# A memory-recurrent transformer block on one core: half-wide partial sums in the memory's output pass, free tile shapes for token projections, new orders

## The chip, the cores and the metric

The kernel runs on one core of a Trainium2 chip. The metric is device time in microseconds, the median of several runs; less is better. Engines are named as in the profile: PE is the matmul engine (PEld its weight loads), DVE the vector engine, ACT the scalar engine, POOL the general one, SP the engine that issues most DMAs.

## What is computed

Two layers over 2048 tokens of width 448, in bfloat16, each an attention block with a recurrent memory and a gated MLP with a relu gate, both with a residual sum:

```python
def _A_ref(x, mem0, Wq, Wk, Wv, Wo, seg_len):        # 16 heads of 256, M = 8, seg_len = 32
    ...
    mem = mem0
    for s in range(n_seg):                            # 64 segments
        xs = x[:, s * seg_len:(s + 1) * seg_len, :].copy()
        h = jnp.concatenate([mem, xs], axis=1)        # 8 memory rows and 32 tokens
        q = jnp.einsum('btd,dhe->bhte', h, Wq)
        ...                                           # k and v likewise
        scores = jnp.einsum('bhqe,bhke->bhqk', q, k) * scale
        scores = jnp.where(mask[None, None], scores, -1000000000.0)
        p = _softmax(scores, axis=-1)
        o = jnp.einsum('bhqk,bhke->bhqe', p, v)
        o = jnp.einsum('bhte,hed->btd', o, Wo)
        mem = o[:, :M, :].copy()
        outs.append(o[:, M:, :])
    return jnp.concatenate(outs, axis=1)
...
x = x + _A_ref(_layernorm(x, axis=-1), A_mem0, A_Wq, A_Wk, A_Wv, A_Wo, A_seg_len)
x = x + _B_ref(_layernorm(x, axis=-1), B_W_gate, B_W_up, B_W_down)
x = x + _A_ref(_layernorm(x, axis=-1), A_mem0, A_Wq, A_Wk, A_Wv, A_Wo, A_seg_len)
x = x + _B_ref(_layernorm(x, axis=-1), B_W_gate, B_W_up, B_W_down)
```

The memory of a segment is the output of the eight memory rows of the segment before. That is a chain of 64 steps in each layer. The weights are the same in both layers.

## The kernel before

**Weights.** Wq and Wk of a head are multiplied into one matrix `A` (448 x 448 a head), Wv and Wo into one matrix `Bsb`, so that a head's scores are h A h' and its output is p h B. This is done once at the start: `transposes` (L1086), `product` (L1104).

**The chain.** `chain(step)` does one step of the recurrence for both layers at once: layer 1 at segment `step`, layer 2 at segment `step - LAG`, with `LAG = 7`. The memory rows of both layers (and, from step 7, 16 rows of tokens of an even tile that "ride" along) are 32 columns of `mT`. One step has these parts in turn:

- `A` times `mT` (L1268, in tiles of 64 x 32 of the PE array), copied to `Usb`;
- `Usb` turned by matmuls with `Selm` (L1444) into `uTm`;
- scores (L1467), softmax (L1477 to L1484), a turn of the probabilities (L1507), and the weighted sum of the segment's rows (L1534 to L1541) into `YTm`: 56 chunks of 128 x 32;
- the **output pass** (L1307): the 56 chunks times the 56 chunks of `Bsb`, four at once in tiles of 128 x 32, so that four partial sums of 32 rows x 448 columns stand in the four quarters of one bank of partitions;
- the four partial sums added: ACT copies the first (L1322), DVE adds the second and the third (L1324) and the fourth (L1325, into `Ohi`), and `twice` (L1205) copies 64 columns of `Ohi` for the rotation of blocks;
- the **column product** (L1350), a small matmul per block with a selection matrix, which turns `Ohi` into columns; `halves` copies these into `mT` for the next step.

In steps before `LAG` another form is used: the pass in 256 and 192 columns, both halves of a two-term split summed by matmuls (L1334, L1341). Step 7 (`step < SPLIT`, `SPLIT = 8`) has the pass in 256 and 192 columns with the sums by ACT and DVE.

**Token work.** Between the parts of the chain stand the tokens of the tiles of 128: `att_group` (queries times `A`, L1626, in tiles of 64 x 128; scores, L1655; softmax; weighted sum, L1537 and L1541; output projection, L1693, 128 x 128 tiles), and the MLP (`glu_units`, L1715, 64 x 128 tiles; `glu_down`, L1733, 128 x 128 tiles). `copy_any` (L278, L281) is the copy out of PSUM that ACT or DVE may do.

**Orders.** Nothing is scheduled at run time. The operations are recorded, and `ORDER`, a list of numbers, says in which order they go and on which engine (the number modulo 5 is the engine); `BANKS` gives the PSUM bank of each. `FILLS` puts matmuls on a scratch tile at some places of PE's order. Each engine runs its list in order, waiting on semaphores for what other engines must have done.

**Tile shapes.** The PE array can be used as one tile of 128 x 128, two of 64 x 128, four of 128 x 32 or eight of 64 x 32; an operation's `mode` names the shape (0: 128 x 128, 1: 128 x 32, 2: 64 x 128, 3: 128 x 64, 4: 64 x 32). The column product may run in mode 0 or 2, according to what stands before and after it:

```python
if o.mode == 5:
    o.mode = mode if mode in (0, 2) else 0 if after and after.mode == 0 else 2
```

Of the kernel before, what the change touches and what calls it, by code (L numbers as in the profile page):

```python
# [7 lines left out]
ALU = mybir.AluOpType  # L8
# [42 lines left out]
class _Sched:  # L51
# [76 lines left out]
    def schedule(self):  # L128
# [27 lines left out]
        for o, after in zip(order["pe"], order["pe"][1:] + [None]):  # L156
            if o.mode == 5:
                o.mode = mode if mode in (0, 2) else 0 if after and after.mode == 0 else 2
            mode = o.mode
# [98 lines left out]
EV = ("act", "dve")  # L258

# [25 lines left out]
def bass_interleave_layers__memory_aug_recurrent_mem_tr__glu_gated_reglu__prompt_kernel(  # L285
# [474 lines left out]
)  # L760
FILLS = {56: (11, 0, 0), 69: (9, 0, 0), 1306: (7, 2, 0), 1461: (46, 1, 1)}
TURN = (
# [1098 lines left out]
```

## Time and profile before

| | |
|---|---|
| median of 3 runs | 1510.02 us (1508.71 to 1512.96) |
| profiled execution | span 1515.3 us from its first to its last instruction; no other time of it is given |
| PE busy | 1478.4 us, 98% of the span, 37579 matmuls |
| DVE busy | 1109.6 us, 73% |
| ACT busy | 841.0 us, 56% |
| granted clock of PE | 0.997 on average |

The profile is of one execution. Each line of a group gives the code line, the engine, the operation, what is written and read, the shape and the count, then busy time and the mean of one in ns, then the engine's idle time before it and who ended it. Lines of the timeline begin with the start and the duration in us. Matmuls are pipelined: the start of the next tells when the array is free, the duration of one includes its passage through the array.

### The profile page before, as it was taken

Reading aid. Unit: us, or ns where it says so; the run is one execution under the profiler, and the core shown is the slowest. Engines: PE = TensorE matmul, PEld = TensorE weight load, DVE = VectorE, ACT = ScalarE, POOL = GpSimd, SP = SyncE. Lnnn points to the kernel's source line nnn. Section 1 sums busy time; section 2 is a strip of 40 time slices with the busy share of each in tenths; the row PEclk is TensorE's granted clock in tenths of the full one; section 3 lists DMA queues with packets and bytes.
Section 4 is the critical chain, followed back from the end, with each engine's and each line's share of the span. In section 5 each row is a group of like instructions: output and inputs, shape, how many; then the busy total and the mean of one; then the engine's idle time right before and its main releaser. Section 6 shows DMA issues by size and latency. Waiting matters only on the chain.

```text
span 1515.3 us, 83381 instructions
## 1 busy us (share of the span) xinstructions
PE 1478.4 (98%) x37579; PEld 1063.1 (70%) x37579; DVE 1109.6 (73%) x3353; ACT 841.0 (56%) x2383; POOL 60.0 (4%) x240
## 2 busy tenths in 40 slices
PE   8999999999999999999999999999999999999998
PEld 6576766667667776677767777677767676677675
DVE  7655768678776878678776778778777878778774
ACT  6755556556565556555655655555555556545542
POOL 1000000000000000000000000000000000000000
PEclk9999999999999999999999999999999999999999
DMA  9831122222222212212122223213222222213211
GB/s 237 194 89 44 28 43 44 44 37 46 46 39 41 45 32 51 42 31 52 44 42 38 44 44 53 40 35 47 47 44 31 52 43 53 39 41 40 47 27 27
DMA packets 239346, 78.20 MB, mean 52 GB/s; under 512 B 212104, under 2 KB 238992, under 8 KB 238992
## 3 DMA queue, kind: packets, MB, share of 16 engines
q1 hardware_dynamic: 238352, 72.60, 25.2%
q8 instruction: 297, 4.87, 1.4%
q14 instruction: 57, 0.47, 0.1%
q10 hardware_dynamic: 640, 0.26, 0.1%
HBM read 17.68 MB, written 1.84 MB: 13 GB/s over the span
## 4 chain that ended last, share of the span: by engine, by line
PE 87%; DVE 6%; DMA 3%; ACT 2%; issue 1%; SPq 1%; DVEq 0%; POOL 0%
PE psG L1626 14%; PE psG L1693 14%; PE psG L1715 11%; PE psC L1307 11%; PE psC L1268 7%; PE psG L1733 6%; PE psG L1268 5%; PE psG L1104 3%; PE psG L1537 2%; PE psG L1655 2%; PE psC L1467 1%; PE psC L1693 1%; PE psC L1444 1%; DMA UR<-Usb 1%; PE psC L1534 1%
## 5 line engine op out<-in xcount | busy, mean ns | idle before, releaser
L1693 PE MATMUL psG<-Bsb,YT 128*128 128x448 bf16 x1232 | 263.8, 353 | 0.0
L278 ACT ACTIVATE Ug<-psG 64x128 bf16<-64x128 f32 (+2 forms) x424 | 152.7, 374 | 73.6 <-PE psG L1626 64.5
L1307 PE MATMUL psC<-Bsb,YTm 128*32 128x448 bf16 (+2 forms) x4088 | 188.0, 335 | 1.0 <-DVE YTm L281 0.5
L1715 PE MATMUL psG<-G,glu 64*128 64x128 bf16 x5866 | 183.6, 216 | 2.6 <-DMA G<-xn 2.4
L1715 PEld LDWEIGHTS psG<-G,glu 64*128 64x128 bf16 x5866 | 170.3, 94 | 14.5 <-issue 8.6
L1626 PE MATMUL psG<-HT,A 64*128 64x128 bf16 x3424 | 175.8, 217 | 0.3 <-ACT Bsb L278 0.3
L1693 PEld LDWEIGHTS psG<-Bsb,YT 128*128 128x128 bf16 x1232 | 107.3, 97 | 89.0 <-issue 7.7
L1268 PE MATMUL psG<-A,mT 64*32 64x448 bf16 x4564 | 158.8, 350 | 2.8 <-issue 1.9
L1626 PE MATMUL psG<-HX,A 64*128 64x128 bf16 x2568 | 149.9, 217 | 0.0
L1307 PEld LDWEIGHTS psC<-Bsb,YTm 128*32 128x32 bf16 x4088 | 101.4, 97 | 67.2 <-DVE YTm L281 3.2
L281 DVE CAST Ug<-psG 64x128 bf16<-64x128 f32 (+2 forms) x277 | 114.9, 427 | 25.3 <-PE psG L1626 21.3
L1268 PE MATMUL psC<-A,mT 64*32 64x448 bf16 x3276 | 128.8, 351 | 1.0 <-issue 0.6
L1626 PEld LDWEIGHTS psG<-HT,A 64*128 64x128 bf16 x3424 | 116.6, 94 | 8.9 <-issue 5.0
L1324 DVE TENSOR_TENSOR Usb<-psC,Usb 32x448 f32<-32x448 f32 (+2 forms) x122 | 74.4, 610 | 63.7 <-ACT Usb L1322 60.9
L278 ACT ACTIVATE YT<-psG 128x448 bf16<-128x448 f32 x217 | 109.3, 538 | 20.3 <-PE psG L1541 20.0
L281 DVE CAST YT<-psG 128x448 bf16<-128x448 f32 x145 | 88.2, 618 | 41.2 <-PE psG L1541 40.4
L1720 ACT ACTIVATE hG<-psG 128x512 bf16<-128x512 f32 (+1 forms) x123 | 66.7, 543 | 81.6 <-PE psG L1715 78.8
L1268 PEld LDWEIGHTS psG<-A,mT 64*32 64x32 bf16 x4564 | 80.5, 92 | 32.3 <-issue 4.0
L1733 PE MATMUL psG<-glu,hG 128*128 128x448 bf16 x448 | 99.8, 353 | 0.0
L1268 PEld LDWEIGHTS psC<-A,mT 64*32 64x32 bf16 x3276 | 64.9, 93 | 45.4 <-ACT mT L278 2.7
L1626 PEld LDWEIGHTS psG<-HX,A 64*128 64x128 bf16 x2568 | 95.2, 94 | 0.0
L1626 PE MATMUL psG<-l,A 64*128 64x128 bf16 x2807 | 94.4, 216 | 0.0
(274 smaller groups left out, 2755.7 us busy)
## 6 DMA issues: line engine op xcount, KB each, us to landing
Bsb<-in_A_Wq_dram SPq DMA_DIRECT2D x6, 384.0 KB
Bsb<-in_A_Wk_dram SPq DMA_DIRECT2D x6, 384.0 KB
Tsb<-Ohi SPq DMA_DIRECT2D x128, 7.0 KB
UR<-Usb SPq DMA_TRANSPOSE x124, 2.9
X<-in_A_x_dram SPq DMA_DIRECT2D x16, 112.0 KB, 5.6
glu<-in_A_Wo_dram SPq DMA_DIRECT2D x4, 448.0 KB
out_dram<-X SPq DMA_DIRECT2D x16, 112.0 KB
glu<-in_B_W_gate_dram SPq DMA_DIRECT2D x14, 112.0 KB
```

The lines of the kernel that those rows point to most:

```text
L278: return E.activation(out, i, ACT.Copy, scale=1.0 if scale is None else scale)
L281: return E.tensor_copy(out, i)
L1104: i = E.matmul(bk.ap()[row0:row0 + mn, 0:D], lhsT=lhs[:, et, m0:m0 + mn], rhs=rhs[:, et, :], start=(et == 0), stop=(et == 1), tile_positio ...
L1268: i = E.matmul(ub[v].ap()[32 * j:32 * j + 32, 0:D], lhsT=self.mT[rw, b, :], rhs=self.A[rw, b, a0:a0 + D], start=(b == 0), stop=(b == 6), t ...
L1307: x = E.matmul(bo.ap()[32 * j:32 * j + 32, 0:d1 - d0], lhsT=self.YTm[:, q, :], rhs=self.Bsb[:, chunks[q], d0:d1], start=(i == 0), stop=(i ...
L1324: s.add("dve", dv_cost(n), lambda E, e, j=j, a_=a_, part=part: E.tensor_tensor(a_, part(j), a_, ALU.add), r=[bo], w=w, part=(j, 0), **P)
L1537: return E.matmul(ps[:, n * q:n * q + n], lhsT=HR[rows, KM + 128 * q:KM + 128 * q + 128], rhs=PT, start=True, stop=True, tile_position=(b, 0))
L1626: i = E.matmul(ub[v].ap()[:, 128 * n:128 * n + 128], lhsT=self.A[rw, b, a0:a0 + 128], rhs=HT[rw, b, :, 0:SEG] if b < 4 else HX[rw, b - 4, ...
L1693: i = E.matmul(bo.ap()[:, 0:D], lhsT=YT[:, c, :], rhs=self.Bsb[:, 14 * g + c, :], start=(g == 0 and c == 0), stop=(g == 3 and c == 13))
L1715: i_ = E.matmul(two[v].ap()[:, 128 * c:128 * c + 128], lhsT=self.Wgu[rw, b, f0:f0 + 128], rhs=G[rw, b, :], start=(b == 0), stop=(b == 6), ...
L1720: s.add("act", 169 + 0.84 * N, lambda E, e, dst=dst, z=two[0], N=N: E.activation(dst, z.ap()[:, 0:N], ACT.Relu), r=[two[0]], w=[("hG", i, ...
L1733: i_ = E.matmul(bk.ap()[:, 0:D], lhsT=hG[:, c, :], rhs=self.Wd[:, c, :], start=(c == 0), stop=(c == NFC - 1))
```

## The change

Four things change. First, the output pass from step 7 on (`out_pass`): a chunk's 448 columns are taken in two halves of 224, by two of the four tiles, so that the bank holds two partial sums of each half, not four of the full width. There are 28 rounds of four 224-wide matmuls in place of 14 of four 448-wide ones. ACT copies one part of each half and DVE adds the other; `twice` follows the first half. Step 7 takes this form too. Second, the output projection of tokens and `glu_down` (mode 6) take the shape that stands before them if that is 128 x 128 or 128 x 32; in the latter each 448-wide matmul becomes four with 32 columns of weights each (`by_rows`). The column product (mode 7) may take 128 x 128, 128 x 32 or 64 x 128. Third, `ORDER`, `BANKS` and `FILLS` are new: the order of all operations, the engine of many copies, and the order of the loads at the start. Fourth, the probabilities' write also names the tile's first clearing as something it comes after.

```diff
-        for o, after in zip(order["pe"], order["pe"][1:] + [None]):
-            if o.mode == 5:
-                o.mode = mode if mode in (0, 2) else 0 if after and after.mode == 0 else 2
+        for o in order["pe"]:
+            if o.mode in FREE:
+                o.mode = mode if mode in FREE[o.mode] else 0
             mode = o.mode
...
+FREE = {6: (0, 1), 7: (0, 1, 2)}
+
+def by_rows(E, mode, out, lhsT, rhs, **k):
+    if mode != 1:
+        return E.matmul(out, lhsT=lhsT, rhs=rhs, **k)
+    for j in range(4):
+        c = slice(32 * j, 32 * j + 32)
+        i = E.matmul(out[c], lhsT=lhsT[:, c], rhs=rhs, tile_position=(0, 32 * j), **k)
+    return i
...
-FILLS = {56: (11, 0, 0), 69: (9, 0, 0), 1306: (7, 2, 0), 1461: (46, 1, 1)}
+FILLS = {12: (50, 7, 0), 22: (9, 1, 0), 54: (5, 3, 0), 70: (4, 6, 0)}
...
-        for d0, d1 in ((0, 256), (256, D)) if step < SPLIT else ((0, D),):
+        if step >= LAG:
+            self.out_pass(chunks, ykeys, P)
+        for d0, d1 in ((0, 256), (256, D)) if step < LAG else ():
...
-            s.add("act", 169 + 0.84 * n, lambda E, e, a_=a_, part=part: E.activation(a_, part(0), ACT.Copy), r=[bo], w=w, **P)
-            for j in (1, 2):
-                s.add("dve", dv_cost(n), lambda E, e, j=j, a_=a_, part=part: E.tensor_tensor(a_, part(j), a_, ALU.add), r=[bo], w=w, part=(j, 0), **P)
-            s.add("dve", dv_cost(n), lambda E, e, a_=a_, o_=o_, part=part: E.tensor_tensor(o_, part(3), a_, ALU.add), r=[bo] + w, ...)
...
+    def out_pass(self, chunks, ykeys, P):
+        s = self.s
+        n = D // 2
+        bo = self.bank("C", "G")
+        for lo, hi in ((0, 10), (10, 20), (20, 28)):
+            def oo(E, e, lo=lo, hi=hi):
+                for i in range(lo, hi):
+                    for j in range(4):
+                        q = 2 * i + j // 2
+                        d0 = n * (j % 2)
+                        x = E.matmul(bo.ap()[32 * j:32 * j + 32, 0:n], lhsT=self.YTm[:, q, :], rhs=self.Bsb[:, chunks[q], d0:d0 + n],
+                                     start=(i == 0), stop=(i == 27), tile_position=(0, 32 * j))
+                return x
+            s.add("pe", (hi - lo) * 96, oo, r=ykeys + self.B_all, w=[bo], alloc=[bo] if lo == 0 else (), mode=1, **P)
+        for g in range(2):
+            a_, o_ = self.Osum[:, n * g:n * g + n], self.Ohi[0:32, 64 + n * g:64 + n * g + n]
+            part = lambda z, g=g: bo.ap()[32 * (g + 2 * z):32 * (g + 2 * z) + 32, 0:n]
+            s.add("act", 169 + 0.84 * n, lambda E, e, a_=a_, part=part: E.activation(a_, part(0), ACT.Copy), r=[bo],
+                  w=[("Usb", 2 * g)], part=(g, 0), **P)
+            s.add("dve", dv_cost(n), lambda E, e, a_=a_, o_=o_, part=part: E.tensor_tensor(o_, part(1), a_, ALU.add), r=[bo, ("Usb", 2 * g)],
+                  w=["Ohi"] if g == 0 else [("Ohi", 256)], part=(g + 2, 0), **P)
+            if g == 0:
+                self.twice(self.Ohi, "Ohi", "Ohi2", P)
...
-                    i = E.matmul(bo.ap()[:, 0:D], lhsT=YT[:, c, :], rhs=self.Bsb[:, 14 * g + c, :], start=(g == 0 and c == 0), stop=(g == 3 and c == 13))
+                    i = by_rows(E, op[0].mode, bo.ap()[:, 0:D], YT[:, c, :], self.Bsb[:, 14 * g + c, :], start=(g == 0 and c == 0), stop=(g == 3 and c == 13))
...
-                    i_ = E.matmul(bk.ap()[:, 0:D], lhsT=hG[:, c, :], rhs=self.Wd[:, c, :], start=(c == 0), stop=(c == NFC - 1))
+                    i_ = by_rows(E, op[0].mode, bk.ap()[:, 0:D], hG[:, c, :], self.Wd[:, c, :], start=(c == 0), stop=(c == NFC - 1))
...
-                      r=[k_(f"E{c}"), k_(f"rc{c}")], w=[k_(f"P{c}")], **P)
+                      r=[k_(f"E{c}"), k_(f"rc{c}"), k_("P")], w=[k_(f"P{c}")], **P)
```

More of the change, by code (lines that the diff above doesn't have):

```diff
@@ L1297, in chain @@
         ykeys = [(k, c, z) for k in ("YTm", "YTr") for c in range(2) for z in (0, 28)]
-        O, acc = self.Ohi, self.Osum
-        for d0, d1 in ((0, 256), (256, D)) if step < SPLIT else ((0, D),):
+        O = self.Ohi
+        if step >= LAG:
+            self.out_pass(chunks, ykeys, P)
+        for d0, d1 in ((0, 256), (256, D)) if step < LAG else ():
             bo = self.bank("C", "G")
             n = d1 - d0
-            for lo, hi in ((0, 5), (5, 10), (10, 14)) if n == D else ((0, 14),):
+            for lo, hi in ((0, 14),):
                 def oo(E, e, lo=lo, hi=hi, bo=bo, d0=d0, d1=d1):
@@ L1310, in chain @@
                 s.add("pe", (hi - lo) * max(n / 2.4 + 3, 100), oo, r=ykeys + self.B_all, w=[bo], alloc=[bo] if lo == 0 else (), mode=1, **P)
-            part = lambda j, bo=bo, n=n: bo.ap()[32 * j:32 * j + 32, 0:n]
-            if step < LAG:
-                hi, lo = (z[:, 64 + d0:64 + d1] for z in self.HL)
-                s.add("act", 169 + 0.84 * n, lambda E, e, hi=hi, bo=bo, n=n: E.activation(hi, bo.ap()[:, 0:n], ACT.Copy), r=[bo], w=[("Hi", d0)], **P)
-                s.add("dve", dv_cost(n), lambda E, e, hi=hi, lo=lo, bo=bo, n=n: E.tensor_tensor(lo, bo.ap()[:, 0:n], hi, ALU.subtract),
-                      r=[bo, ("Hi", d0)], w=[("Lo", d0)], **P)
-                if d0 == 0:
-                    for w, k in zip(self.HL, ("Hi", "Lo")):
-                        self.twice(w, (k, 0), k + "2", P)
-                continue
-            a_, o_, w = acc[:, d0:d1], O[0:32, 64 + d0:64 + d1], [("Osum", z) for z in (0, 256) if d0 <= z < d1] + [("Usb", 0), ("Usb", 2)]
-            s.add("act", 169 + 0.84 * n, lambda E, e, a_=a_, part=part: E.activation(a_, part(0), ACT.Copy), r=[bo], w=w, **P)
-            for j in (1, 2):
-                s.add("dve", dv_cost(n), lambda E, e, j=j, a_=a_, part=part: E.tensor_tensor(a_, part(j), a_, ALU.add), r=[bo], w=w, part=(j, 0), **P)
-            s.add("dve", dv_cost(n), lambda E, e, a_=a_, o_=o_, part=part: E.tensor_tensor(o_, part(3), a_, ALU.add), r=[bo] + w, w=["Ohi"] * (d0 == 0) + [("Ohi", 256)] * (d1 == D),
-                  part=(3, 0), **P)
+            hi, lo = (z[:, 64 + d0:64 + d1] for z in self.HL)
+            s.add("act", 169 + 0.84 * n, lambda E, e, hi=hi, bo=bo, n=n: E.activation(hi, bo.ap()[:, 0:n], ACT.Copy), r=[bo], w=[("Hi", d0)], **P)
+            s.add("dve", dv_cost(n), lambda E, e, hi=hi, lo=lo, bo=bo, n=n: E.tensor_tensor(lo, bo.ap()[:, 0:n], hi, ALU.subtract),
+                  r=[bo, ("Hi", d0)], w=[("Lo", d0)], **P)
+            if d0 == 0:
+                for w, k in zip(self.HL, ("Hi", "Lo")):
+                    self.twice(w, (k, 0), k + "2", P)
         bc_ = self.bank("C", "G")
@@ L1344, in chain @@
         else:
-            self.twice(O, "Ohi", "Ohi2", P)
             def cols(E, e):
@@ L1349, in cols @@
                 for k in range(4):
-                    i = E.matmul(pk()[:, k, :], lhsT=block(O, k)[0:n], rhs=self.Sel16[0:n, :], start=True, stop=True, **at)
+                    i = by_rows(E, op.mode, pk()[:, k, :], block(O, k)[0:n], self.Sel16[0:n, :], start=True, stop=True, **at)
                 return i
-            op = s.add("pe", 4 * 28, cols, r=["Ohi", ("Ohi", 256), "Ohi2", "Sel16"], w=[bc_], alloc=[bc_], mode=5, **P)
+            op = s.add("pe", 4 * 28, cols, r=["Ohi", ("Ohi", 256), "Ohi2", "Sel16"], w=[bc_], alloc=[bc_], mode=7, **P)
         self.halves(self.mT[:, :, 0:16], pk, 16, bc_, "mTm", ("mTh",), P=P)
@@ L1501, in middle @@
                 s.add("dve", 239, lambda E, e, c=c, b=b: E.tensor_scalar(Pv[:, b, 0:L], m["E"][:, c, 0:L], m["st"][:, 4 + c:5 + c], None, op0=ALU.mult),
-                      r=[k_("Em"), k_("rc")], w=[k_(f"P{c}")], **P)
+                      r=[k_("Em"), k_("rc"), k_("P")], w=[k_(f"P{c}")], **P)
         if m["n"] == "r":
```

9 lines of the change are left out of this document (4 added, 5 removed), and 1075 rows, old and new, of tables (BANKS, ORDER).

## The prediction, before the result

> **What bounds the kernel now.** I read the page's sums first, then busy time by stretch of the span, then what the matmul engine waited for, and last one step of the recurrence in order of time. From the page:
>
> ```profile
> span 1515.3 us, 83381 instructions
> PE 1478.4 (98%) x37579; PEld 1063.1 (70%) x37579; DVE 1109.6 (73%) x3353; ACT 841.0 (56%) x2383; POOL 60.0 (4%) x240
> PE 87%; DVE 6%; DMA 3%; ACT 2%; issue 1%; SPq 1%; DVEq 0%; POOL 0%
> ```
>
> PE is busy for 98% of the span and carries 87% of the chain that ended last. All PE work added is therefore paid, and all that can be won is in the 36.9 us (1515.3 - 1478.4) in which PE idles. Where these lie is in the sums by stretch (PE busy is the second number after the stretch):
>
> ```profile
> 0.00:6.00 6.00, 0.49 (x6) 0.52 (x7) 4.56 (x17) 1.28 (x1) 5.38 (x19) 1.00 0.66 186
> 6.00:70.00 64.00, 63.33 (x740) 39.96 (x738) 48.05 (x111) 50.31 (x104) 2.23 (x6) 1.00 0.95 229
> 70.00:400.00 330.00, 316.57 (x8516) 227.67 (x8516) 228.57 (x713) 180.10 (x538) 12.23 (x50) 0.99 0.25 48
> 400.00:1480.00 1080.00, 1067.52 (x27784) 773.98 (x27777) 815.22 (x2485) 602.11 (x1726) 40.12 (x166) 1.00 0.23 42
> ```
>
> 5.5 us go before the first matmul. The weight products until 70 us lose 0.7, the early steps until 400 us lose 13.4, the long middle loses 12.5, and the rest, 4.8, comes after 1480 us, nearly all behind the last matmul. So some 26.6 us stand between matmuls. The clock is granted in full (0.99 to 1.00), so the clock explains nothing. Who ends PE's waits:
>
> ```profile
> PE psC L1350 <- DVE Ohi L1205: 2.6, 3, 2.0
> PE psG L1715 <- DMA G<-xn: 2.4, 2, 2.2
> PE psG L1268 <- issue: 1.9, 2, 1.2
> PE psG L1467 <- ACT uTm L278: 1.8, 5, 0.6
> PE psC L1534 <- DMA Tr<-Pr: 1.7, 3, 0.8
> PE psC L1467 <- DVE uTr L281: 1.6, 3, 0.9
> ```
>
> No single wait is large. Most are in the recurrence (L1350, L1467, L1268), and DVE ends more of them than ACT.
>
> **The change part by part.** The sum is made on the span of the profiled execution, 1515.3 us. The median of the runs is 1510.02, 0.35% less; I scale the sum by 1510.02 / 1515.3 = 0.9965.
>
> *Output pass, PE.* From step 7 on, 63 steps, 14 rounds of four 448-wide matmuls become 28 rounds of four 224-wide ones. The steps before show both shapes. A steady step, and below it an early one whose pass runs as 14 rounds of 256 and 14 rounds of 192, which is 28 rounds of 224 on average:
>
> ```profile
> 802.41 2.83 PE L1307 MATMUL psC<-Bsb,YTm 128*32 128x448 bf16 x56
> ...
> 805.17 3.30 PE L1715 MATMUL psG<-G,glu 64*128 64x128 bf16 x112
> 805.29 0.53 ACT L1322 ACTIVATE Usb<-psC 32x448 f32<-32x448 f32 x1 [1.52 <-PE psC L1307]
> 805.86 1.27 DVE L1324 TENSOR_TENSOR Usb<-psC,Usb 32x448 f32<-32x448 f32 x2 [1.98 <-ACT Usb L1322]
> ...
> 807.16 0.62 DVE L1325 TENSOR_TENSOR Ohi<-psC,Usb 32x448 bf16<-32x448 f32 x1
> ...
> 807.85 0.24 POOL L1205 COPY Ohi<-Ohi 128x64 bf16<-128x64 bf16 x1 [11.17 <-DVE Ohi L1325]
> 808.31 0.20 PE L1350 MATMUL psC<-Sel,Ohi 64*128 64x16 bf16 x2
> ```
> ```profile
> 71.65 2.87 PE L1307 MATMUL psC<-Bsb,YTm 128*32 128x256 bf16 x112
> 74.45 0.40 PE L1626 MATMUL psG<-HT,A 64*128 64x128 bf16 x8
> ```
>
> From the pass's start to the next start: 805.17 - 802.41 = 2.76 us for 14 wide rounds, 74.45 - 71.65 = 2.80 for 28 narrow ones. That is 0.04 more in each of 62 steps (step 7 was split already): **+2.5 us**. The doubled weight loads hide.
>
> ```profile
> L1307 PEld LDWEIGHTS psC<-Bsb,YTm 128*32 128x32 bf16 x4088 | 101.4, 97 | 67.2 <-DVE YTm L281 3.2 <-issue 0.7 <-DVE uTr L281 0.4
> ```
>
> One load lasts 97 ns, yet 112 loads and 112 matmuls pass in 2.80 us, 25 ns a pair. [...]
>
> *Tile shapes.* Full-width projections in 128x128 tiles:
>
> ```profile
> 1487.76 5.47 PE L1693 MATMUL psG<-Bsb,YT 128*128 128x448 bf16 x28
> 1493.07 0.92 PE L1733 MATMUL psG<-glu,hG 128*128 128x448 bf16 x4
> ```
>
> (1493.07 - 1487.76) / 28 = 0.190 us each. Fourteen rounds at 0.190 are 2.66, and the pass above took 2.76 with one change of tile shape behind it: a change of shape costs 0.10 us. Token projections that now run as four 32-column matmuls are one such 448-wide round, 0.190 again: nothing. (The new order does this for 221 of 1888.) What it is for is fewer changes of shape, but the two instruction orders, counted, have 552 before and 581 after: 29 x 0.10 = **+2.9 us**. In eight steps the small column product after the pass runs as 16 matmuls of 32 columns in place of four. Its cost lies between nothing (four at once) and 12 more at the 25 ns of a pair above, 0.3 us; half of it, times 8: **+1.2 us** (0 to 2.4).
>
> *Behind the output pass.* Before, ACT copies the first part (0.53), DVE adds three (1.27 and 0.62), POOL doubles 64 columns: from the pass's end, 802.41 + 2.83 = 805.24, to the column product at 808.31, 3.07 us. After, ACT copies two half-wide parts, DVE adds one to each, and the doubling needs the first half alone. The step that was split shows such widths:
>
> ```profile
> 182.88 0.37 ACT L1322 ACTIVATE Usb<-psC 32x256 f32<-32x256 f32 x1 [0.52 <-PE psC L1307]
> 183.32 0.87 DVE L1324 TENSOR_TENSOR Usb<-psC,Usb 32x256 f32<-32x256 f32 x2
> ...
> 184.68 0.32 ACT L1322 ACTIVATE Usb<-psC 32x192 f32<-32x192 f32 x1 [1.43 <-DVE Ohi L1325]
> ...
> 185.03 0.74 DVE L1324 TENSOR_TENSOR Usb<-psC,Usb 32x192 f32<-32x192 f32 x2 [0.17 <-ACT Usb L1322]
> ```
>
> Halfway between 256 and 192: ACT 0.345, DVE 0.40. One copy and two adds, the second copy beside the first add, with the 0.05 (805.24 to 805.29), 0.04 and 0.22 (808.09 to 808.31) seen between steps: 0.345 + 2 x 0.40 + 0.3 = 1.45 us. The recurrence is 1.6 us shorter per step, and DVE's load falls by 62 x 1.89 - 63 x 0.80 = 67 us, while ACT's rises by 63 x 0.69 - 62 x 0.53 = 11.
>
> *What that is worth.* PE didn't stand still for these 3.07 us: the order put token work there. Pricing the matmuls that stand between the pass and the column product (0.190 for a full one, and so on), I count a median of 3.3 to 3.6 us before and 2.1 to 2.6 after, so the order takes back some 1.1 of the 1.6. That work now stands in the other gaps of the step; before the next step's first product the quarter point rises from 1.1 to 1.5 us. So the gain isn't 63 x 1.6 = 101 us; it is at most what PE idles between matmuls, 26.6. Some 22 of these can go at the most (26.6 less the DMA rows of the list, 2.4 and 1.7, which stay); nothing is the least, if other work is late next. I take a little more than the middle, **-13 us**: wider gaps in nearly every place, and the engine that ends most waits lighter by 6% (67 of 1109.6).
>
> *The start.* The new order puts 59 filling matmuls before the first weight transposes, where PE waited 5.5 us anyway:
>
> ```profile
> 5.51 0.80 PE L1086 MATMUL psG<-ident,Bsb 128*128 128x128 bf16 x6 [5.51 <-DMA Bsb<-in_A_Wq_dram]
> 6.96 1.38 PE L183 MATMUL psC<-warm 128*128 128x128 bf16 x11
> ```
>
> Eleven took 1.38 us, 0.11 each with the last one's drain; 59 at 0.09 last from 1 to about 6.3 us, so the transposes start 0.8 later, then run without the 20 fills that stood among them. Against that, SP's queue now has three DMA transposes of Wv ahead of the last loads of Wq and Wk:
>
> ```profile
> 31.58 4.41 SPq L1046 DMA_TRANSPOSE glu<-in_A_Wv_dram  x1
> 10.00:20.00 10.00, 9.66 (x125) 6.67 (x125) 7.26 (x17) 7.26 (x15) 0.07 (x1) 1.00 1.10 309
> 30.00:40.00 10.00, 10.00 (x115) 6.58 (x113) 7.20 (x18) 8.11 (x16) 0.00 (x0) 1.00 1.07 188
> ```
>
> Plain loads came at 309 GB/s; in the stretch of the transposes 188. The PE work that needed 7.7 MB delivered now needs 10.7, at about 35 us. At 309 for 9.3 MB and 188 for 1.4, these have landed at 38 us at the earliest and 43 if SP is held up for each as here, 4.4 us. I put the start at **+1.5 us** (-1.5 to +6).
>
> *Sum.* 2.5 + 2.9 + 1.2 + 1.5 - 13 = -4.9: 1510.4 on the profile's scale, times 0.9965: **1505 us**, 0.33% less. 0.3%, 4.5 us, is about what a measurement of this kernel can tell from no change.
>
> **The rivals.**
> 1. *The waits move.* The order shortened the gap as the recurrence shortened; another releaser (ACT's share, which rises, or a transfer) is late next, and PE idles as long as before. For it: the list of waits is flat, with ACT, DMA and issue in it. Against: the gaps grow elsewhere too. Place: the recurrence's matmuls in steps 7 to 69. Price: only 2.5 + 2.9 + 1.2 + 1.5 = +8.1 is left, 1523.4, so 1518 us. It ends slower when less than 3.6 us of idle time goes (8.1 - 4.5).
> 2. *The start starves.* The weights land at 43 us, PE loses 8 us: +6.5 on my sum, 1516.9, so 1511.6. For it: the byte counts; against: other products were put there as cover.
> 3. *DVE's relief goes further.* All 22 us go: 1501.4, so 1496 us. For it: DVE ends most waits; against: the early steps' idle time is partly lack of token work.
> 4. *Weight loads come to light.* If the second half's loads didn't overlap, 14 rounds of 0.097 in 62 steps are 84 us: 1594, so 1589. The 2.80 us row speaks against it. [...]
>
> **How the numbers follow.** Forecast 0.35 (its own range 1500 to 1510: 0.20 faster, 0.15 the same), rival 1 0.27 (0.24 slower, 0.03 the same), rival 2 0.13 (0.02, 0.06, 0.05), rival 3 0.24 (faster), rival 4 0.01 (slower). Faster 0.46, same 0.24, slower 0.30. The range runs from 1492 (rival 3 with the cheap ends: 0 for the column product, -1.5 for the start) to 1523 (rival 1 with the dear ones, 2.4 and 6); it leaves out rival 4 and the combination of rivals 1 and 2.
>
> **What would show it.** In the profile after: the pass's matmuls 224 wide, its start to the next start 2.80 us; one ACT copy and one DVE add to each half, 0.35 and 0.40; from the pass to the column product 1.5 us where PE has nothing else; DVE busy near 1043 us, ACT near 852; PE idle after 70 us near 13 us rather than 26; the first weight transposes near 6.3 us and no idle over 3 us before 75. I am wrong if PE's idle time after 70 us stays over 22 us (rival 1), if PE's list of waits shows several us on the weights (rival 2), or if PE's busy time rises by much more than 7 us (the tile shapes or rival 4).

## The result, and the profile after

The changed kernel takes 1535.86 us (median; 1531.35 to 1538.69), the kernel before beside it 1510.69: the ratio is 1.0169 [1.0151, 1.0187]. It is slower, by 1.7%, where 1505 us was forecast; the range ended at 1523. Run once more later it took 1543.08 us, ratio 1.0199 [1.0179, 1.0219].

The page of the changed kernel: the span, busy time by engine, one of the DMA queues (packets, MB, share of 16 engines' span), and the chain by engine.

```profile
span 1534.8 us, 91834 instructions
...
PE 1494.1 (97%) x41805; PEld 1149.3 (75%) x41805; DVE 1021.3 (67%) x3281; ACT 846.4 (55%) x2442; POOL 60.4 (4%) x249
...
q8 instruction: 330, 5.41, 1.4%
...
PE 92%; DMA 3%; DVE 1%; issue 1%; ACT 1%; SPq 1%; POOL 0%
```

The same queue on the page of before:

```profile
q8 instruction: 297, 4.87, 1.4%
```

PE is still the bound. It has 4226 matmuls more than before (41805 against 37579), but only 15.7 us more busy time, for 19.5 us more span. The row to see, and one that I had passed over, is the queue that carries instructions: 330 packets of 16 KB in place of 297.

The sums by stretch of the changed kernel (PE busy is the second number after the stretch, the granted clock the third from the end):

```profile
6.00:70.00 64.00, 53.18 (x563) 34.63 (x562) 36.76 (x91) 37.42 (x81) 2.97 (x7) 0.96 0.94 221
70.00:400.00 330.00, 321.04 (x9352) 241.29 (x9358) 214.93 (x690) 184.86 (x551) 14.53 (x59) 0.99 0.23 48
400.00:1480.00 1080.00, 1064.46 (x30661) 829.62 (x30647) 738.87 (x2417) 602.65 (x1760) 39.39 (x168) 1.00 0.23 43
```

Until 70 us PE idles 10.8 us, where before it idled 0.7. After that it idles 9.0 and 15.5 us, 24.5 in all, against 13.4 and 12.5 before: nothing gained. PE's waits, the largest first (us in total, times, longest):

```profile
PE psG L1453 <- issue: 2.9, 6, 0.8
PE psG L1271 <- issue: 2.7, 1, 2.7
PE psC L1271 <- DVE A L291: 2.6, 1, 2.6
PE psG L1289 <- issue: 2.3, 1, 2.3
PE psG L1567 <- DVE YTm L292: 1.9, 4, 0.8
```

Before, one of the six largest was "issue", a wait for which the profile shows no releaser. Now three of five are; but two of these three, at L1271 and L1289, are single stops of the start, before 75 us, and their matmuls have a semaphore to wait for. So the list alone doesn't tell. I added up PE's idle time between matmuls, pauses over 40 ns beyond the passing of the matmuls' columns and the time of a change of tile shape, by whether the matmul that ends it has a semaphore to wait for:

```
                        before 75 us        after 75 us
                        all waits     semaphore   no semaphore
before                     3.2          38.6          8.4
changed                   17.4          30.9         22.6
difference               +14.2          -7.7        +14.2
```

The sum is +20.7 of the +19.5 us of span; the rest, -1.2, holds among others the work added and the 4.5 us by which the first matmul, a filling one, starts sooner (at 0.99 us, not 5.51). The split depends a little on how a pause is counted: from start to start, with 0.09 us taken off for a change of shape, the differences are +14.5, -10.2 and +13.3. So two things were lost, of like size: the start, and pauses with nothing to wait for. The relief that was forecast is there too, but smaller.

### The profile page after: what moved, and what is told of

Same layout as the page of the kernel before. It is cut to its first block, busy times and chain, and to the rows that moved or that the text cites. A ratio compares the mean times of both kernels' runs of the same rounds, so it can differ in the third digit from the quotient of the medians.

```text
span 1534.8 us, 91834 instructions
## 1 busy us (share of the span) xinstructions
PE 1494.1 (97%) x41805; PEld 1149.3 (75%) x41805; DVE 1021.3 (67%) x3281; ACT 846.4 (55%) x2442; POOL 60.4 (4%) x249
## 4 chain that ended last, share of the span: by engine, by line
PE 92%; DMA 3%; DVE 1%; issue 1%; ACT 1%; SPq 1%; POOL 0%
PE psG L265 14%; PE psG L1827 13%; PE psG L1453 10%; PE psG L1916 9%; PE psG L1567 8%; PE psC L265 5%; PE psC L1827 4%; PE psC L1453 3%; PE psC L1567 3%; PE psC L1916 3%; PE psG L1738 3%; PE psG L1856 2%; PE psG L268 2%; PE psG L1289 2%; PE psG L1668 2%; PE psG L1645 1%
## 5 line engine op out<-in xcount | busy, mean ns | idle before, releaser
L1453 PE MATMUL psG<-A,mT 64*32 64x448 bf16 x5852 | 194.8, 350 | 3.5 <-issue 2.9
L265 PE MATMUL psG<-Bsb,YT 128*128 128x448 bf16 x831 | 177.4, 352 | 0.0
L1453 PEld LDWEIGHTS psG<-A,mT 64*32 64x32 bf16 x5852 | 101.6, 92 | 62.2 <-issue 10.8
L1567 PE MATMUL psG<-Bsb,YTm 128*32 128x224 bf16 x5264 | 136.2, 259 | 2.9 <-DVE YTm L292 1.9
L1567 PEld LDWEIGHTS psG<-Bsb,YTm 128*32 128x32 bf16 x5264 | 123.0, 97 | 9.3 <-issue 2.5
L265 PEld LDWEIGHTS psG<-Bsb,YT 128*128 128x128 bf16 x831 | 72.4, 97 | 57.6 <-issue 2.6
L289 ACT ACTIVATE YT<-psG 128x448 bf16<-128x448 f32 x177 | 92.9, 542 | 16.8 <-PE psG L1742 12.5
L289 ACT ACTIVATE Usb<-psG 128x448 bf16<-128x448 f32 x126 | 66.2, 543 | 61.0 <-PE psG L1453 52.1
L1827 PEld LDWEIGHTS psG<-l,A 64*128 64x128 bf16 x2359 | 86.9, 94 | 2.2 <-issue 1.2
L1916 PE MATMUL psC<-G,glu 64*128 64x128 bf16 x1428 | 82.3, 216 | 0.5 <-issue 0.3
L1576 DVE TENSOR_TENSOR Ohi<-psG,Usb 32x224 bf16<-32x224 f32 x94 | 36.5, 388 | 68.7 <-ACT Usb L1574 65.5
L1574 ACT ACTIVATE Usb<-psG 32x224 f32<-32x224 f32 x94 | 32.6, 347 | 83.1 <-PE psG L1567 67.2
```

Source lines behind the costliest of these rows:

```text
L265: return E.matmul(out, lhsT=lhsT, rhs=rhs, **k)
L289: return E.activation(out, i, ACT.Copy, scale=1.0 if scale is None else scale)
L1453: i = E.matmul(ub[v].ap()[32 * j:32 * j + 32, 0:D], lhsT=self.mT[rw, b, :], rhs=self.A[rw, b, a0:a0 + D], start=(b == 0), stop=(b == 6), t ...
L1567: x = E.matmul(bo.ap()[32 * j:32 * j + 32, 0:n], lhsT=self.YTm[:, q, :], rhs=self.Bsb[:, chunks[q], d0:d0 + n], start=(i == 0), stop=(i == ...
L1574: s.add("act", 169 + 0.84 * n, lambda E, e, a_=a_, part=part: E.activation(a_, part(0), ACT.Copy), r=[bo], w=[("Usb", 2 * g)], part=(g, 0) ...
L1576: s.add("dve", dv_cost(n), lambda E, e, a_=a_, o_=o_, part=part: E.tensor_tensor(o_, part(1), a_, ALU.add), r=[bo, ("Usb", 2 * g)], w=["Oh ...
```

## What the pauses without a semaphore are

One of them, in a kernel that differs from before in the output pass alone (below, e_narrow), in order of time on PE:

```profile
766.43 0.22 PE L1539 MATMUL psG<-Tx,HR 40*128 40x128 bf16 x1
768.19 0.34 PE L1539 MATMUL psG<-Tx,HR 40*128 40x128 bf16 x5 [1.54 <-issue]
768.31 0.27 PE L1543 MATMUL psG<-Tx,HR 40*128 40x64 bf16 x4
```

The pause is inside one operation, between two of its matmuls: their data are there. So I looked at instructions as a thing that must arrive. In the traces each matmul is two (weight load and matmul), each wait that stands by itself is one; for the changed kernel 2 x 41805, 880 waits and 4 others are 84494, and 330 packets of 16 KB came: 330 x 16384 / 84494 = 63.99 bytes an instruction (before 297 x 16384 / 75995 = 64.03). At 64 bytes these are 330.05 pieces of 16 KB, of 256 instructions each. Numbering PE's instructions in its order gives each pause a place within its piece of 256. The first eight pauses of 0.15 us and more in e_narrow, worked out from its trace:

```
pause ends at us   length   instruction no.   no. modulo 256   since the last fetch ended
     112.6          0.29         4291              195                 1.42
     116.8          0.39         4547              195                 1.57
     218.1          0.16         9923              195                 1.20
     366.9          0.17        18371              195                 1.35
     455.9          1.04        23235              195                 1.66
     459.7          0.33        23491              195                 1.31
     498.5          0.64        25795              195                 1.49
     513.1          0.28        26563              195                 1.46
```

All 38 of them stand at 195 or 196, whatever the line, the tile shape or the operands; so do all 46 of the changed kernel. (Below this place is called the piece's end; the numbers begin with the first instruction counted, so where in the 16 KB it lies isn't known.) And each ends 1.2 to 1.7 us (in a few cases up to 2.6) after a packet of the instruction queue had ended, which itself took 0.9 to 1.8 us. By these rows PE waited for its own instructions. In the median a fetch of the changed kernel starts some 200 instructions, 100 matmuls, ahead of this place, but only some 150, 75 matmuls, where PE then stood; from its start until PE went on it took 2.2 to 3.2 us in most cases. A hundred matmuls of 128x32 tiles and 224 columns pass in 100 x 23.5 ns = 2.35 us, of 64x128 and 128 columns in 2.7 us: about as long, and 75 of them are too soon. A hundred of the wide pass take 4.8 us, longer than those 3.2: there, by these numbers, the supply can catch up. The change took this breathing space out of each step.

How many such pieces PE holds at a time, no run here shows.

## The experiments

The theory A of the expectations is this supply of instructions. Ratios are to the kernel before in the same rounds.

**1. The narrow pass alone.**

```diff
-for i in range(lo, hi):
+w = 224 if d1 - d0 == D else d1 - d0
+for r in range(lo * D // w, hi * D // w) if w == 224 else range(lo, hi):
+    i, c = r % 14, d0 + 224 * (r // 14)
     for j in range(4):
         q = 4 * i + j
-        x = E.matmul(bo.ap()[32*j:32*j+32, 0:d1-d0], ..., rhs=self.Bsb[:, chunks[q], d0:d1], ...)
+        x = E.matmul(bo.ap()[32*j:32*j+32, c-d0:c-d0+w], ..., rhs=self.Bsb[:, chunks[q], c:c+w], ...)
```

> The kernel before, with only the output pass of steps 8 to 69 issued as 28 rounds of 224 columns into the same four partial sums (first half of the columns, then second): same products, order, additions and start as before; 41051 matmuls in place of 37579. Theory A (instruction supply: the matmul engine outruns the fetches of its own instructions, 16 KB for 127 pairs of weight load and matmul, so that more and smaller matmuls stall it with no semaphore to wait for): 2.5 us of work as forecast, and the stalls without a semaphore after 75 us rise from 8 us to some 18, so 1521 us (1517 to 1526). Theory B (the new orders cost it all, the narrow pass is as cheap as its row says): 2.5 us and nothing else, 1513 us, stalls without a semaphore stay under 10.

Measured: 1533.89 us (1530.41 to 1536.23), ratio 1.0144 [1.0126, 1.0162], 21 us. Its page:

```profile
span 1528.6 us, 90325 instructions
...
PE 1487.3 (97%) x41051; PEld 1138.7 (74%) x41051; DVE 1109.6 (73%) x3353; ACT 841.0 (55%) x2383; POOL 60.1 (4%) x240
...
q8 instruction: 324, 5.31, 1.4%
```

Pauses without a semaphore after 75 us: 19.7 us, 17.3 of them at the pieces' ends. This is theory A, and more than it expected: its range ended at 1526. The same sums, additions, order and start as before, only twice as many matmuls of half the width, cost nearly all of what the changed kernel lost.

**2. The new pass and sums in the order of before.** The eight operations of the new pass and sums take the places of the old ones; projections stay in 128x128 tiles.

```diff
-ORDER = (the new order)
+ORDER = (that of before; second copy and add behind the first add; one add fewer)
-    if o.mode in FREE: ...
+    (the column product's mode by the rule of before; projections in mode 0)
```

> The new output pass and its sums (two column halves of two partial sums) in the order of before, with the start of before and all projections in 128x128 tiles. Same 41051 matmuls as the kernel with the narrow pass alone. Theory A: the stalls of that kernel, less what the shorter recurrence saves in an order not made for it, 2 to 5 us: 1518 us (1514 to 1523). Theory B (the new orders cost it all): the sums alone gain, 1500 to 1510 us.

Measured: 1533.67 us, 1.0130 [1.0106, 1.0154], a miss for theory A (1514 to 1523) as well as B: beside experiment 1, no gain from the shorter sums shows. DVE's load did fall as forecast, to 1039.8 us, and ACT's rose to 852.7:

```profile
PE 1489.0 (97%) x41051; PEld 1140.4 (74%) x41051; DVE 1039.8 (68%) x3286; ACT 852.7 (56%) x2445; POOL 60.6 (4%) x241
```

**3. The changed kernel with the start of before.**

```diff
-ORDER = (the new order)
+ORDER = (the first 493 entries of the order of before, then the rest of the new one)
-FILLS = {12: (50, 7, 0), 22: (9, 1, 0), 54: (5, 3, 0), 70: (4, 6, 0)}
+FILLS = {56: (11, 0, 0), 69: (9, 0, 0)}
```

> The changed kernel with the start of before (weights, first norms and first fillers in the old order, up to the last weight product), the rest in the new order. If the late first rows and the transposing loads cost the start 13 us, these go: 1523 us (1520 to 1526), the last weight product near 69.5 us rather than 82, and the stalls without a semaphore after 75 us stay near 22 us. If the recurrence waits later for something else anyway, most of the 13 us come back as waits: over 1530.

Measured: 1533.6 us, 1.0140 [1.0122, 1.0158]: 2 us less than the changed kernel in its own, earlier rounds, or 4.4 us by the ratios (1.0140 and 1.0169). The profile had the start back (4.8 us of waits before 75 us, not 17.4). This was a miss that had to be settled (experiment 9).

**4. The changed kernel with projections in 128x128 tiles.**

```diff
-FREE = {6: (0, 1), 7: (0, 1, 2)}
+FREE = {6: (0,), 7: (0, 1, 2)}
```

> The changed kernel with all token projections kept in 128x128 tiles: 747 matmuls fewer, 19 changes of tile shape more (1.9 us). Theory A (instruction supply): some 6 fetches fewer and less dense stretches, stalls without a semaphore fall by 2 to 4 us, so 1534 us (1531 to 1537). If four 32-column matmuls are as good as one full one, the shape changes alone count: 1538 us, stalls without a semaphore unchanged.

Measured: 1533.79 us, 1.0141 [1.0122, 1.0161], where theory A said 1534 and the shape changes alone 1538. But the pauses did not fall (25.1 us at the pieces' ends in this profile), and the changed kernel's own runs lie 7 us apart. So it is open what the 32-column projections cost; more than nothing was not shown.

**5. More instructions, the same matmuls.** Waits for semaphores that were reached long ago, behind each wide matmul of the pass but the last; four such waits are counted as two instructions, two of one semaphore as one.

```diff
+for e in ("dve", "act", "pool", "pe"):     # the other kernel: "dve" twice
+    E.wait_ge(s.sems[e], 1)
```

> The kernel before, with its 56 wide matmuls of the output pass (steps 8 to 69) untouched, but behind each of them two instructions that only wait for semaphores reached long ago: 2 x 55 x 62 = 6820 matmul-engine instructions of 64 bytes more, so that its instructions fill 323.5 pieces of 16 KB, against 296.9 before and 324.0 with the narrow pass alone. Theory A (instruction supply): the pass now has as many instructions per us as the narrow one, so the stalls without a semaphore rise from 6 to some 17 us, all at the same place within a 16 KB piece, and the time is 1522 to 1535 us. Rival (narrow matmuls and doubled weight loads cost in themselves): 1513 us, no new stalls, unless the pass itself becomes longer, which its start to the next start shows (2.76 us before).

> The same with one such instruction behind each wide matmul: 3410 more, 310.2 pieces. Theory A: less than half of the loss of the kernel with two, since 100 matmuls then outrun a fetch more seldom: 1514 to 1521 us. Rival: 1513 us, no new stalls.

Measured: 2153.94 and 1786.94 us. One pass, with one and with two such instructions to a matmul:

```profile
910.28 7.35 PE L1308 MATMUL psC<-Bsb,YTm 128*32 128x448 bf16 x56
```
```profile
901.76 13.03 PE L1308 MATMUL psC<-Bsb,YTm 128*32 128x448 bf16 x56
```

The pass lasts 7.35 and 13.03 us, not 2.83: in this dense row a wait cost some 80 ns even when it was met ((1786.94 - 1513.14) / 3410; 94 ns with two, (2153.94 - 1513.14) / 6820). That hid what was sought; on the supply of instructions these runs say nothing.

**6. The new order with the old pass and sums.**

```diff
-ORDER = (that of before)
+ORDER = (its first 493 entries, then the new order; the three old adds where the new two stood)
```

> The output pass and sums of before (14 wide rounds, three additions) in the new order, with the start of before: 37526 matmuls, 604 changes of tile shape (52 more than before, 5 us by 0.1 us each). Theory A: with the wide pass the stalls at the pieces' ends are as before, 6 to 8 us; the recurrence is longer than this order was made for, so waits for semaphores stay near the 38 us of before: 1512 to 1520 us. If the new order itself costs the time, it stays over 1525 us.

Measured: 1562.01 us, 1.0326 [1.0312, 1.0341]. The pauses at the pieces' ends are down to 3.5 us, as theory A says for the wide pass. But the forecast time was a miss; PE waits for the sums:

```profile
PE psG L1489 <- POOL Ohi L1344: 26.9, 30, 3.2
PE psC L1489 <- POOL Ohi L1344: 9.7, 11, 1.6
```

36.6 us go in 41 waits of the column product for the doubled columns (L1344 is `twice` in that kernel). The new order puts less work behind the pass; it is of use only with the short sums.

**7. The kernel before, once more.** No edit.

> The kernel before once more, unchanged, for a second profile: by theory A its stalls without a semaphore lie at the same place within the 16 KB pieces as in the first profile, and their sum, 5.9 us there, moves by a few us from one execution to the next, as the fetches do.

Measured: 1512.72 us, 0.9999 [0.9983, 1.0015]; at the pieces' ends 7 pauses of 3.6 us together, 11 of 5.6 in the first profile.

**8. Fewer instructions elsewhere.** The token path's matmuls of 128 columns become wider and fewer, with the same columns in all, in the kernel before, the one with the narrow pass, and the changed one. These kernels leave out a part of the computation: the queries' matmuls read weights in place of the memory rows and tokens, and the 224-wide results of gate/up overlap, so the output is not that of the layers. Loads, copies, orders and waits stay.

```diff
-for b in range(7):                       # gate/up; the queries too, from A
+o = min(128 * c, N - 224)
+for b in range(4):
     for v in range(2):
-        E.matmul(two[v].ap()[:, 128*c:128*c+128], ..., rhs=G[rw, b, :], start=(b == 0), stop=(b == 6), ...)
+        E.matmul(two[v].ap()[:, o:o+224], ..., rhs=(G as one row)[rw, 224*b:224*b+224], start=(b == 0), stop=(b == 3), ...)
```

> The kernel before, with the token path's matmuls of 64x128 tiles (queries and gate/up) issued as four of 224 columns in place of seven of 128: the same 896 columns, 6720 matmuls fewer (30859), 53 fewer fetches of 16 KB. Those of the queries read weights in place of the memory rows and those of gate/up overlap their outputs, so the token output isn't the reference's. By itself: the stalls without a semaphore (4 to 6 us before) nearly go, 1500 to 1512 us.

> The same wide token matmuls, and the output pass as 28 rounds of 224 columns into four partial sums: 34331 matmuls, fewer than the kernel before has. Theory A (instruction supply): with the token work less dense the narrow pass no longer outruns the fetches; against the kernel with wide token matmuls and the wide pass it costs its 2.5 us of work and up to 4 us of stalls, not 21. Rival (the narrow matmuls and their doubled weight loads cost by themselves): 18 us or more above that kernel, as without the wide token matmuls.

> The changed kernel with the same wide token matmuls (35085 matmuls). Theory A: without the stalls the new order's lower waits and its late start remain, 4 to 14 us above the kernel before with wide token matmuls, and the stalls without a semaphore fall from 19 to under 6 us. Rival: 20 us or more above it.

Measured: 1502.05, 1507.37 and 1511.67 us. Busy time and the instruction queue of the first, and of the second:

```profile
PE 1466.4 (98%) x30859; PEld 1043.0 (70%) x30859; DVE 1108.2 (74%) x3353; ACT 839.7 (56%) x2383; POOL 60.5 (4%) x240
...
q8 instruction: 244, 4.00, 1.1%
```
```profile
PE 1469.0 (98%) x34331; PEld 1116.4 (74%) x34331; DVE 1108.3 (74%) x3353; ACT 839.9 (56%) x2383; POOL 60.5 (4%) x240
...
q8 instruction: 271, 4.44, 1.3%
```

This decides it. The narrow pass is the same in both pairs, with all its matmuls and weight loads; where the token work leaves room it costs 5.3 us (1507.37 - 1502.05), 2.6 of them busy time of PE, 1.9 pauses at the pieces' ends. In the full kernel it cost 21. The rival, that narrow matmuls cost 18 us or more by themselves, is out.

**9. The start, from both sides.** The kernel before with the new start; then, since it was open why experiment 3 gained so little, the changed kernel with the old start and the wide token matmuls, the new sums in the old order with these, and experiment 3 and the changed kernel once more on one chip. The edits are those of 3, 8 and 2 combined; for the first, which also has the fills of the new start and the fourth part of the change:

```diff
-ORDER = (that of before)
+ORDER = (the first 487 entries of the new order, then the rest of that of before)
```

> The kernel before with the new start (weights, first norms and fillers in the new order up to the last weight product), the rest as before. If the 13 us that the start loses on the matmul engine stay lost: 1526 us (1523 to 1528). If later slack gives most of it back, as the changed kernel with the old start hints (13 us off the start, 2 us off the time): 1515 to 1519 us, with fewer waits for semaphores after 75 us than the 36 to 38 us of before.

> The changed kernel with the start of before and the wide token matmuls (token output not the reference's, as in the other kernels with them): nearly no stalls at the pieces' ends. If the late start is lost for good and only the stalls hid that (the changed kernel with the old start gained 2 us, not 13), it lies 10 to 13 us below the changed kernel with wide token matmuls (1511.7): 1499 to 1502 us. If the recurrence or a transfer takes the time back later, stalls or not: 1506 us or more.

> The new output pass and sums in the order and with the start of before, with the wide token matmuls. Against the narrow pass with the old sums and wide token matmuls (1507.4) it shows what the shorter sums are worth in an order not made for them, without the stalls: if waits fall with the recurrence, 1500 to 1504 us; if the order gives each matmul its place anyway, 1507 us.

> The changed kernel with the start of before once more, beside the changed kernel on one chip. 13 us off the start were expected to be 13 us off the time; the first runs gave 2. If the start's 13 us go through: 1521 to 1526 us. If most of it comes back: 1530 to 1535 us, and the profile shows where: more stalls at the pieces' ends or more waits for semaphores after 75 us than the changed kernel has (22.6 and 30.9 us).

> The changed kernel once more, unchanged, for a second profile and more runs beside the one with the old start: 1533 to 1538 us, last weight product near 82 us, stalls at the pieces' ends 16 to 22 us.

Measured: 1531.91, 1496.6, 1507.68, 1533.0 and 1543.08 us. The first, the second and the last lie outside what was expected, the first above, the second below, the last above. Side by side, the old start is worth 10.1 us to the changed kernel (1543.08 - 1533.0), and 15 with wide token matmuls (1511.67 - 1496.6, on two chips; by the ratios 0.9980 and 0.9901, 12 us). In the kernel before the new start costs 1.24% [1.04%, 1.43%], some 19 us (16.8 by the medians), of which 5 to 8, according to the profile of before, are new waits for semaphores after 75 us; some 4 of them lie between 75 and 120 us, behind the place where the two orders are joined. So the 2 us of experiment 3 were a comparison across rounds, between which the changed kernel itself moved by 7 us. The two profiles of the pair, until 70 us, with the old start and with the new:

```profile
6.00:70.00 64.00, 63.34 (x737) 39.94 (x736) 48.15 (x111) 50.28 (x104) 2.23 (x6) 1.00 0.92 230
```
```profile
6.00:70.00 64.00, 55.45 (x624) 36.10 (x623) 39.25 (x96) 38.47 (x84) 3.06 (x8) 0.95 0.94 224
```

PE idles 0.7 us there with the old start and 8.6 with the new, at a granted clock of 1.00 and 0.95.

All pauses at the pieces' ends (after 75 us, of 0.15 us and more), worked out as above; another way of counting moves a row by up to 2 us:

```
                                        pieces of   number   us together
                                          16 KB
before                                     297      11, 7     5.6, 3.6   (two profiles)
before, new start                          297        9         4.8
new order, old pass and sums               296        7         3.5
narrow pass alone                          324       38        17.3
new pass and sums, old order               324       44        19.5
changed, old start                         329     40, 42    19.8, 22.6
changed, projections 128x128               324       47        25.1
changed                                    330     46, 52    18.8, 25.5
wide token matmuls: before                 244        1         0.2
    narrow pass                            271        5         2.1
    new pass and sums, old order           271        8         4.8
    changed                                277        9         4.2
    changed, old start                     277       11         4.4
```

The second profile of the changed kernel, span 1541.2, is 6.4 us longer than the first, and its pauses are 6.7 us longer. That the scatter of these kernels is that of their fetches is not shown by this one pair: the two profiles of the changed kernel with the old start have spans of 1527.8 and 1527.4 and pauses 2.8 us apart. No version with the whole computation was faster than the kernel before.

## Why the prediction was wrong, step by step

*Output pass, PE: +2.5.* The pass itself was priced rightly: in the median of its 63 steps it takes 2.80 us from its start to the next start, as forecast. In a step of the changed kernel:

```profile
582.34 2.87 PE L1567 MATMUL psC<-Bsb,YTm 128*32 128x224 bf16 x112
...
585.02 1.13 PE L268 MATMUL psG<-Bsb,YT 128*32 128x448 bf16 x20
585.26 0.35 ACT L1574 ACTIVATE Usb<-psC 32x224 f32<-32x224 f32 x1 [0.54 <-PE psC L1567]
...
585.64 0.39 DVE L1576 TENSOR_TENSOR Ohi<-psC,Usb 32x224 bf16<-32x224 f32 x1 [0.32 <-ACT Usb L1574]
...
586.08 0.35 ACT L1574 ACTIVATE Usb<-psC 32x224 f32<-32x224 f32 x1
586.08 0.24 POOL L1390 COPY Ohi<-Ohi 128x64 bf16<-128x64 bf16 x1 [13.98 <-DVE Ohi L1576]
...
586.46 0.39 DVE L1576 TENSOR_TENSOR Ohi<-psC,Usb 32x224 bf16<-32x224 f32 x1
...
587.06 0.25 PE L265 MATMUL psC<-Sel,Ohi 128*128 128x16 bf16 x4
```

585.02 - 582.34 = 2.68 us with no change of shape behind it, so 2.8 with one; the doubled weight loads hide (112 of them, 97 ns each in the mean, pass with the matmuls in these 2.68 us), and rival 4 is out. (Its price counted one load a round, 84 us; with the 56 added loads of each step exposed it would have been 56 x 0.097 x 62 = 337 us. Neither showed.) PE's busy time did rise by 15.7 us where these three terms make 6.6, which was named as a sign of the tile shapes or rival 4. Most of the excess is likely of another kind: a matmul's record lasts some 0.16 us longer than its columns pass (0.216 us for 128 columns that pass in 0.053), so that much of each pause behind it counts as busy, and 35 more pauses (46 against 11) make 5.7 us of these 9.1 by this estimate. **The step that failed is this term all the same**: it counted the pass's own duration and not the 112 instructions more per step. With them it is 21 us (experiment 1), and 5.3 where token work leaves room (experiment 8). The trace of before had it: five of its pauses in the 64x32 matmuls, 3.3 us together, had no semaphore and stood at that same place, and its list of waits showed "issue" at L1268. I put that down as one more small wait.

*Tile shapes, +2.9, and the column product, +1.2.* No run has them alone, but the traces have their rows. The matmuls counted in order have 552 changes of shape before and 581 after, and a change with no semaphore cost 0.09 to 0.10 us in the trace of before. In the changed kernel a round of four 32-column matmuls takes 0.189 us, like a full one, and the 16 small matmuls of the column product take 0.19 us where four take 0.10: 0.7 us in eight steps. So as time on PE these terms hold. What their instructions cost besides (three more for each of 221 rounds of the projections) was not shown either way (experiment 4).

*Behind the pass, 1.45 us.* The second add ends 586.46 + 0.39 - 585.21 = 1.64 us behind the pass's end, in the median 1.63, where before the last add ended after 2.75; the column product comes 1.66 at the earliest. The eviction times were right (0.35 and 0.39), but the second copy isn't beside the first add, it waits for it:

```profile
L1576 DVE TENSOR_TENSOR Ohi<-psG,Usb 32x224 bf16<-32x224 f32 x94 | 36.5, 388 | 68.7 <-ACT Usb L1574 65.5 <-issue 2.1
L1574 ACT ACTIVATE Usb<-psG 32x224 f32<-32x224 f32 x94 | 32.6, 347 | 83.1 <-PE psG L1567 67.2 <-DVE Ohi L1576 15.6
```

The kernel's bookkeeping lets the readers of one bank go one after the other, and the copy has that add ahead of it: 15.6 us of ACT's idle time ended with the add. The loads of DVE and ACT were forecast at 1043 and 852; with the sums alone they are 1039.8 and 852.7 (experiment 2), and in the changed kernel, whose order also moves copies, 1021.3 and 846.4.

*What that is worth, -13.* Semaphore waits after 75 us fell by 7.7 us, or by 2.4 from the second profile of before (35.9) to that of the changed kernel (33.5). The mechanism was right and the split of it wrong. With wide token matmuls, where the pauses are few, the shorter sums alone bring nothing (1507.68 against 1507.37), the new order with its tile shapes on top of them 11.1 (1507.68 - 1496.6). It needs both; the order without the sums is 49 us slower than before (experiment 6). With the full token work this gain is gone (1533.67 against 1533.0 to 1533.6). That the pauses make the recurrence late again is a likely reason; it was argued only.

*The start, +1.5 (-1.5 to +6).* Mis-sized: 10 us or more. I counted bytes until the last weights land. PE was stopped well before that, one stop at a time:

```profile
11.63 7.01 SPq L1231 DMA_TRANSPOSE glu<-in_A_Wv_dram  x1
...
18.17 0.63 DVE L1757 BATCH_NORM_STATS2 lnst<-X 128x6 f32<-128x448 bf16 x1 [3.87 <-DMA X<-in_A_x_dram]
18.71 0.61 DVE L291 TENSOR_SCALAR A<-psC 128x448 bf16<-128x448 f32 x1
...
19.38 0.51 PE L1271 MATMUL psC<-ident,Bsb 128*128 128x128 bf16 x6 [2.65 <-DVE A L291]
...
31.95 5.08 SPq L1231 DMA_TRANSPOSE glu<-in_A_Wv_dram  x1
35.22 0.50 PE L1271 MATMUL psG<-ident,Bsb 128*128 128x128 bf16 x6 [2.72 <-issue]
```

At 11.63 SP's queue is held 7.01 us by one transposing load. The first rows of x land at 18.17, DVE's list has the norm of these rows next and stands 3.87 us, the copy of `A` behind it is late, and PE waits for that copy until 19.38. Stops at 35.22, 45.65 (on Wq) and 67.84 follow. For the first of these this profile shows no releaser; in the second profile of this kernel the same matmuls start at 35.42, after 4.68 us that ended with a load of Wq. What ended the last stays open. The last weight product starts at 82.0 us and not 69.8, and the granted clock falls to 0.96 over this stretch. This is rival 2 in kind (a late start), though not by its mechanism alone, and with 12 us in place of 8. The step that failed asked when the last byte lands, and never which engine's list stands behind each load.

*The rivals.* Rival 1's sign was there, PE idle after 70 us over 22 (24.5), but with a releaser that it did not name: ACT's share of the chain fell from 2% to 1%, and no wait on a transfer of data stands among PE's five largest; instructions were late. The range ended at 1523 because it left rivals 1 and 2 together out. Together they make 1515.3 + 8.1 + 6.5 = 1529.9 and so 1524.5 us, still 11 us short: the late instructions had no place in any rival. Whether the change would gain without the pauses and with the old start, as forecast, is not shown: both with wide token matmuls, 1496.6 against 1502.05 is -5.5 us, but on two chips, and the ratios to the kernel before on each, 0.9901 [0.9884, 0.9919] and 0.9913 [0.9897, 0.9929], don't differ beyond their intervals (-1.8 us). The sum without its start was 2.5 + 2.9 + 1.2 - 13 = -6.4.

## What to carry to other kernels

Count instructions as a load of their own: when a change makes more and smaller matmuls, look at the instruction queue's packets and at pauses that end with "issue" inside an operation, and compare the time of a hundred matmuls with that of a fetch (here 2.35 us in the narrow pass, with 2.2 to 3.2 us from a fetch's start until PE went on). As in this kernel, a wide stretch in a dense stream (4.8 us for a hundred matmuls) may be what lets the supply catch up, so it isn't free to split: here 21 us. A load moved ahead of another is to be followed into each engine's list: whoever stood in order behind it paid, here DVE 3.87 us and PE 2.65.

## What was not expected of the hardware

A fetch of 16 KB of instructions took 0.9 to 1.8 us and PE, where it stood, mostly went on 1.2 to 1.7 us after its end; it stood at instruction 195 or 196 of 256 in the kernel before, in that of experiment 1 and in the changed one. The price of the matmuls by column stayed the same at half the width (a pass of 112 with 224 columns took 2.68 us, one of 56 with 448 columns 2.76 with the 0.10 of a change of shape behind it); the loss lay not in the matmul but in its instructions. A wait that was met cost PE 80 to 94 ns when one or two stood behind each matmul of a dense row, while 64x128 matmuls with a single wait in front stood 52 to 53 ns behind the pair before, like those without (trace of before).
